# Raw attention products on quarters of the array, with loads, stores and order rearranged

## The chip, the core and the metric

The kernel runs on one core of a Trainium2 chip. The metric is the device time of one execution in microseconds (us). Three executions of the kernel before took 323.3, 323.69 and 323.8 us, a median of 323.69. The engines of the core are called as in the profile: PE is TensorE (the array that multiplies matrices), PEld its loading of weights, DVE is VectorE, ACT is ScalarE, POOL is GpSimd, and SP is SyncE, which here only issues DMAs. ACT and POOL issue DMAs too. Each engine executes its own instructions in the order in which the program lists them, and waits where one needs what another engine has not delivered.

## The reference

Batch 8, 8 heads, 576 tokens, head size 64, so 512 channels. Everything is float32 in the kernel; the weights arrive as float64 and are narrowed on the chip.

```python
def _attn_ref(q, k, v, g_norm):
    kv = np.einsum('bhsd,bhse->bhde', k, v)
    out = np.einsum('bhsd,bhde->bhse', q, kv)
    rms = np.sqrt(np.mean(out * out, axis=-1, keepdims=True) + 1e-06)
    return (out / rms * g_norm).astype(np.float32)

# x = the heads side by side: (8, 576, 512)
def _moe_ref(x, w_val, conv_w, w_out):
    # gate_pre[s] = sum over k of conv_w[k] * x[s - 4 + k], a causal filter of 5 taps per channel
    gate = 1.0 / (1.0 + np.exp(-gate_pre))
    val = x @ w_val
    return (gate * val @ w_out).astype(np.float32)
```

## The kernel before

**Tiling.** For each of the 8 batches the 576 tokens are cut into four chunks of 128 (numbers 0 to 3) and a tail of 64 (number 4, also written NJ). Heads are taken in four pairs hp; a pair's two heads fill the 128 partitions, r = 0 the lower 64 and r = 1 the upper 64.

**The steps of a batch.** kv_product multiplies k and v into a PSUM tile, 64 by 64 for each head. kv_copy (ACT) puts the result into kv_bd, a tile of 128 by 128 for each pair of heads with the two heads' 64 by 64 blocks on the diagonal and zeros, written once at the start, elsewhere. raw_product multiplies a chunk of q (transposed, in qT, as weights) by kv_bd: one matmul for each pair of heads, 128 columns each. square (ACT) squares the chunk, sums (DVE) adds over each head, powers (POOL) takes the power -1/2, and normalise (for batches 1 to 7 eight ACT instructions, one for each head) scales the chunk from PSUM to SBUF. turn_x and keep_x, or turn_blocks and move_blocks, transpose it into xT. gate_start, gate_tap and gate_end make the gate from xT, val_product or val_fast the val product (val_fast in the seven products of a fast scheme on halves), gated their product, and out_product or fast_product the output, which keep_out or fast_keep takes to SBUF and store writes to memory.

**Order.** PLAN (line 19) is the whole order, written out as one string by a planner that ran beforehand: the last loop of the kernel calls the step named by each piece, so a step's instructions go to the end of their engines' queues in this order. tail_and_kv is the raw product of a batch's tail with kv_product of the next batch. keep_warm n is n matmuls of the identity into a spare piece of PSUM, put where PE would have nothing to do.

**PSUM.** Its eight banks are shared out in line 228, `BANKS = {"kv": 1, "raw": 2, "tp": 1, "mm": 4}`. A raw chunk takes one bank of the two called raw (for batch 0 partly of mm), so that one chunk can be multiplied while the one before is still read. turn_x uses tp. In the last fast products the two raw banks hold the sums called cb and a (out_bank, line 727).

**Queues.** SP issues nearly all loads and stores. For batch 0, load_half puts the two halves of v and the first half of k on ACT's queue and the second half of k on SP's; load_q_rows and load_tails (four DMAs, lines 305 to 310) are on SP's. POOL issues the DMAs of g_norm and conv_w, and those of move_blocks. set_up (line 258) clears, on POOL, those parts of the four tail tiles that stay zero: `for pair in tails`, eight memsets. store_last writes the last two chunks, the even one through SP, the odd one through ACT, four DMAs each.

Of the kernel before, what the change touches and what calls it, by code (L numbers as in the profile page):

```python
# [15 lines left out]
P = 128  # L16
# [3 lines left out]
load_half k 0 0; stage_weight cw 0; load_q_rows 0 0; load_half v 0 0; load_q_rows 0 1; load_tails 0;  # L20
load_half v 0 1; warm_up; keep_warm 16; turn_q_rows 0 0; load_half k 0 1; turn_q_rows 0 1; sort_q 0 0;
turn_q_rows 0 2; stage_weight wval 0; sort_q 0 1; stage_weight wval 1; turn_q_rows 0 3; sort_q 0 2;
turn_q_rows 0 4; load_q_rows 1 0; keep_warm 1; kv_product 0 0; load_q_rows 1 1; load_half k 1 0;
narrow_weight cw 0 0; narrow_weight cw 0 1; load_half v 1 0; narrow_weight cw 0 2; load_tails 1;
narrow_weight cw 0 3; sort_q 0 3; narrow_weight cw 0 4; keep_warm 5; kv_product 0 1; narrow_weight cw 0 5;
sort_q 0 4; narrow_weight cw 0 6; narrow_weight cw 0 7; turn_cw; kv_copy 0; narrow_weight wval 0 0;
narrow_weight wval 0 1; load_half k 1 1; keep_warm 3; raw_product 0 3; load_half v 1 1; narrow_weight wval 1 0;
raw_product 0 2; keep_cw; stage_weight wval 2; square 0 3; stage_weight wval 3; narrow_weight wval 0 2;
raw_product 0 4; sums 0 3; stage_weight wout 0; square 0 2; raw_product 0 1; powers 0 3;
narrow_weight wval 1 1; sums 0 2; square 0 4; narrow_weight wval 0 3; keep_warm 2; turn_q_rows 1 0; square 0 1;  # L30
powers 0 2; normalise 0 3; narrow_weight wval 1 2; sums 0 4; sort_q 1 0; keep_warm 2; turn_x 0 3; sums 0 1;
turn_q_rows 1 1; powers 0 4; keep_x 0 3; normalise 0 2; narrow_weight wval 1 3; powers 0 1; turn_x 0 2;
normalise 0 4; narrow_weight wval 0 4; turn_q_rows 1 2; keep_x 0 2; narrow_weight wval 1 4; turn_x 0 4;
normalise 0 1; keep_x 0 4; narrow_weight wval 1 5; sort_q 1 1; keep_warm 3; raw_product 0 0; halo 0;
narrow_weight wval 1 6; turn_x 0 1; narrow_weight wval 1 7; square 0 0; turn_q_rows 1 3;
narrow_weight wval 0 5; sort_q 1 2; sums 0 0; keep_x 0 1; turn_q_rows 1 4; narrow_weight wval 0 6; powers 0 0;
sort_q 1 3; kv_product 1 0; load_q 2 0; narrow_weight wval 0 7; sort_q 1 4; narrow_weight wval 2 0;
kv_product 1 1; narrow_weight wval 2 1; normalise 0 0; narrow_weight wval 2 2; narrow_weight wval 3 0;
val_product 0 0 1; load_half v 2 1; kv_copy 1; load_q 2 1; narrow_weight wval 2 3; narrow_weight wval 3 1;
narrow_weight wval 2 4; turn_x 0 0; raw_product 1 3; narrow_weight wval 2 5; keep_x 0 0;  # L40
narrow_weight wval 2 6; keep_val 0 0 1; raw_product 1 2; load_half k 2 0; square 1 3; narrow_weight wval 2 7;
gate_start 0 0; load_half k 2 1; val_product 0 1 1; sums 1 3; load_tails 2; narrow_weight wval 3 2;
gate_tap 0 0 3; powers 1 3; square 1 2; gate_start 0 1; sums 1 2; val_product 0 0 0; keep_val 0 1 1;
turn_q 2 0; narrow_weight wval 3 3; powers 1 2; load_half v 2 0; normalise 1 3; gate_tap 0 1 3;
stage_weight wout 2; val_product 0 1 0; gate_tap 0 1 2; load_q 2 2; narrow_weight wout 0 0; keep_val 0 0 0;
narrow_weight wval 3 4; gate_start 0 2; raw_product 1 1; turn_q 2 1; narrow_weight wout 0 1; gate_tap 0 2 3;
turn_x 1 3; square 1 1; load_q 2 3; val_product 0 2 1; narrow_weight wout 0 2; sums 1 1; keep_x 1 3;
gate_tap 0 0 2; powers 1 1; normalise 1 2; gate_tap 0 1 1; val_product 0 2 0; gate_tap 0 0 1;
narrow_weight wval 3 5; normalise 1 1; narrow_weight wval 3 6; turn_x 1 2; gate_tap 0 0 0; raw_product 1 0;
keep_x 1 2; narrow_weight wval 3 7; tail_and_kv 1; square 1 0; gate_tap 0 1 0; keep_val 0 2 1; gate_tap 0 2 2;  # L50
gate_end 0 0; gate_end 0 1; sums 1 0; keep_val 0 1 0; gate_tap 0 2 1; narrow_weight wout 0 3; powers 1 0;
turn_x 1 1; gated 0 0; load_half k 3 0; kv_copy 2; val_product 0 3 1; stage_weight wout 1;
narrow_weight wout 0 4; square 1 4; keep_x 1 1; load_q 3 0; narrow_weight wout 2 0; normalise 1 0; sums 1 4;
turn_q 2 2; powers 1 4; val_product 0 3 0; narrow_weight wout 0 5; turn_q 2 3; gate_start 0 3; load_q 3 1;
normalise 1 4; narrow_weight wout 0 6; turn_x 1 0; gate_tap 0 3 3; raw_product 2 3; keep_x 1 0;
narrow_weight wout 0 7; keep_val 0 2 0; turn_x 1 4; square 2 3; gate_tap 0 3 2; raw_product 2 2; keep_x 1 4;
stage_weight wout 3; sums 2 3; narrow_weight wout 2 1; val_product 1 0 1; load_half k 3 1; gated 0 1;
narrow_weight wout 2 2; powers 2 3; load_tails 3; gate_tap 0 2 0; square 2 2; narrow_weight wout 2 3;
val_sums 0; val_product 1 0 0; keep_val 0 3 1; sums 2 2; keep_val 1 0 1; keep_val 0 3 0;
narrow_weight wout 1 0; powers 2 2; normalise 2 3; narrow_weight wout 2 4; load_half v 3 1; val_product 1 1 1;  # L60
load_half v 3 0; gate_tap 0 3 1; load_q 3 2; gate_tap 0 3 0; narrow_weight wout 1 1; narrow_weight wout 2 5;
gate_end 0 2; turn_blocks 2 3; raw_product 2 1; narrow_weight wout 1 2; turn_q 3 0; val_product 1 1 0;
square 2 1; narrow_weight wout 2 6; keep_val 1 0 0; load_q 3 3; narrow_weight wout 1 3; sums 2 1;
normalise 2 2; narrow_weight wout 2 7; val_product 1 2 1; powers 2 1; turn_q 3 1; narrow_weight wout 1 4;
gate_end 0 3; load_q 4 0; val_sums 1; raw_product 2 0; normalise 2 1; gated 0 2; val_product 1 2 0;
narrow_weight wout 3 0; gated 0 3; narrow_weight wout 3 1; narrow_weight wout 1 5; square 2 0; turn_blocks 2 2;
tail_and_kv 2; narrow_weight wout 3 2; sums 2 0; keep_val 1 1 1; narrow_weight wout 3 3;
narrow_weight wout 1 6; powers 2 0; turn_blocks 2 1; gate_start 1 0; narrow_weight wout 3 4; keep_val 1 1 0;
keep_val 1 2 1; turn_q 3 2; val_product 1 3 1; halo 1; square 2 4; load_half v 4 1; kv_copy 3;
narrow_weight wout 1 7; load_q 4 1; normalise 2 0; sums 2 4; gate_tap 1 0 3; powers 2 4; val_product 1 3 0;  # L70
turn_q 3 3; normalise 2 4; narrow_weight wout 3 5; load_tails 4; narrow_weight wout 3 6; raw_product 3 3;
gate_start 1 3; narrow_weight wout 3 7; gate_start 1 2; turn_x 2 4; turn_blocks 2 0; raw_product 3 2;
keep_x 2 4; gate_tap 1 0 2; square 3 3; move_blocks 2 3; out_product 0 3; square 3 2; load_half k 4 0;
gate_tap 1 2 3; keep_val 1 3 1; load_half v 4 0; gate_tap 1 0 1; keep_val 1 3 0; keep_val 1 2 0; sums 3 3;
gate_tap 1 0 0; powers 3 3; sums 3 2; gate_end 1 0; out_product 0 1; gate_tap 1 2 2; keep_out 0 3; powers 3 2;
gate_tap 1 3 3; normalise 3 3; store 0 3; gated 1 0; gate_tap 1 3 2; move_blocks 2 2; normalise 3 2;
gate_tap 1 2 1; load_half k 4 1; raw_product 3 1; load_q 4 2; gate_tap 1 3 1; out_product 0 2; gate_start 1 1;
turn_blocks 3 3; square 3 1; gate_tap 1 2 0; keep_out 0 1; sums 3 1; gate_tap 1 3 0; powers 3 1;
gate_tap 1 1 3; raw_product 3 0; keep_out 0 2; gate_tap 1 1 2; move_blocks 2 1; out_product 0 0; store 0 2;
normalise 3 1; gate_tap 1 1 1; gate_tap 1 1 0; gate_end 1 2; turn_q 4 0; store 0 1; halo 2; gate_end 1 1;  # L80
val_sums 2; gated 1 1; tail_and_kv 3; keep_out 0 0; load_q 4 3; gated 1 2; gate_end 1 3; gated 1 3;
move_blocks 2 0; turn_blocks 3 2; turn_q 4 1; out_product 0 4; kv_copy 4; turn_blocks 3 1; square 3 4;
load_q 5 0; square 3 0; weight_sums 0; sums 3 4; sums 3 0; powers 3 4; turn_q 4 2; out_product 0 5; powers 3 0;
load_half k 5 0; normalise 3 4; val_sums 3; store 0 0; turn_q 4 3; keep_out 0 4; weight_sums 1; normalise 3 0;
# [104 lines left out]
def kernel(  # L189
# [68 lines left out]
    def set_up():  # L258
# [4 lines left out]
        for pair in tails:  # L263
            for t in pair:
                nc.gpsimd.memset(t[T:P, 0:HP], 0.0)
                nc.gpsimd.memset(t[0:T, HP:H], 0.0)
        for t in kv_bd:
            nc.vector.memset(t[:], 0.0)
# [238 lines left out]
    def heads(c):  # L507
        return H if c < NJ else H // 2
# [315 lines left out]
```

## Time and profile before

The profile is of one execution, which took 324.43 us as a whole; its span, from the first to the last instruction, is 322.6 us. The clock granted to PE was 1.000 over the span.

| | us | instructions |
|---|---|---|
| median of three runs | 323.69 | |
| profiled execution | 324.43 | |
| span in the profile | 322.6 | 6073 |
| PEld busy | 223.2 | 2049 |
| ACT busy | 191.8 | 535 |
| POOL busy | 146.3 | 185 |
| raw products (L500), full array, PE | 33.5 | 256 |
| raw products of tails (L500), half the columns, PE | 5.3 | 64 |
| keep_warm (L432), PE | 10.7 | 64 |
| powers (L528), POOL | 74.0 | 40 |
| normalise on ACT (L539) | 55.5 | 252 |

How to read the views: a row of the groups names line, engine, operation, what is written and read, and the shape, then x and the number of instructions, then the busy time in us and the mean of one in ns, then idle time before them and what ended it. For PE the shape begins with rows*columns of the array that the weights fill. A line of the chain in time order has the start, the length and what the end of the program was waiting for then; consecutive instructions of a kind are merged. In the slices each digit is the busy share of a fortieth of the span in tenths.

### The profile page before, as it was taken

How to read it: one execution, taken by the hardware profiler on the slowest of the kernel's cores; microseconds unless marked ns; L12 is line 12 of the kernel's file. 1: busy time of each engine (PE TensorE's matmuls, PEld its weight loads, DVE VectorE, ACT ScalarE, POOL GpSimd, SP SyncE). 2: the span in 40 equal slices, each digit the busy share in tenths (PEclk: the TensorE clock that was granted, in tenths of full speed). 3: DMA queues.
4: the chain of work that ended last, by engine and by line, in shares of the span. 5: the costliest groups of instructions: out<-in, count | busy, mean ns of one | idle time of the engine just before them, and what ended most of it. 6: DMA issues, size and time to landing. Idle time of an engine off the chain costs nothing.

```text
span 322.6 us, 6073 instructions
## 1 busy us (share of the span) xinstructions
PE 313.4 (97%) x2049; PEld 223.2 (69%) x2049; DVE 246.2 (76%) x430; ACT 191.8 (59%) x535; POOL 146.3 (45%) x185
## 2 busy tenths in 40 slices
PE   8899999899999999999999999999999999999994
PEld 8788888688656577667767675686545676877652
DVE  1149799899989889989897999798748379764511
ACT  1467898999767758495767565656743443341311
POOL 6037254455678578427682943279549000000000
PEclk9999999999999999999999999999999999999999
DMA  8998896995978789688948682223146211112323
GB/s 271 319 335 286 217 294 184 322 305 131 284 194 235 208 253 238 176 259 204 247 108 257 189 249 74 67 65 85 41 114 171 50 33 35 25 40 52 81 66 98
DMA packets 43647, 55.35 MB, mean 172 GB/s; under 512 B 14934, under 2 KB 33366, under 8 KB 43616
## 3 DMA queue, kind: packets, MB, share of 16 engines
q1 hardware_dynamic: 38624, 46.81, 52.5%
q0 software_dynamic: 3168, 6.32, 7.8%
q10 hardware_dynamic: 1824, 1.84, 1.9%
q8 instruction: 16, 0.26, 0.4%
q14 instruction: 15, 0.12, 0.2%
HBM read 39.21 MB, written 9.44 MB: 151 GB/s over the span
## 4 chain that ended last, share of the span: by engine, by line
PE 89%; DMA 4%; ACT 3%; POOL 2%; DVE 1%; ACTq 0%; issue 0%; POOLq 0%
PE out L685 26%; PE va L654 15%; PE raw L500 10%; PE val L604 7%; PE vc L654 7%; PE kv L443 5%; PE out L692 4%; PE a L749 4%; PE vb L654 4%; PE cb L749 3%; DMA v<-in_v_dram 2%; POOL rt L528 2%; DMA vl<-in_v_dram 2%; PE qTps L482 1%; ACT x L539 1%; PE xTps L554 1%
## 5 line engine op out<-in xcount | busy, mean ns | idle before, releaser
L528 POOL TENSOR_TENSOR rt<-ss,mhalf 128x8 f32<-128x8 f32 (+1 forms) x40 | 74.0, 1856 | 85.2 <-DVE ss L522 85.1
L592 DVE SCALAR_TENSOR_TENSOR gate<-xT,cwT,gate 128x576 f32<-128x576 f32 x128 | 101.4, 813 | 9.4 <-ACT gate L586 7.7
L685 PE MATMUL out<-wout,gv 128*128 128x512 f32 x192 | 85.3, 594 | 0.0
L539 ACT ACTIVATE x<-raw,rt 128x64 f32<-128x64 f32 x252 | 55.5, 338 | 17.7 <-POOL rt L528 17.5
L685 PEld LDWEIGHTS out<-wout,gv 128*128 128x128 f32 x192 | 35.9, 190 | 39.5 <-issue 37.7
L575 POOL DMA_DIRECT2D xT<-y x96 | 53.1, 559 | 16.4 <-PE xTps L554 7.5
L500 PEld LDWEIGHTS raw<-kvbd,qT 128*128 128x128 f32 (+1 forms) x320 | 35.7, 180 | 7.0 <-issue 2.7
L500 PE MATMUL raw<-kvbd,qT 128*128 128x128 f32 (+1 forms) x320 | 38.5, 278 | 0.0
L604 PE MATMUL val<-xT,wval 128*128 128x288 f32 x128 | 32.6, 408 | 0.0
L522 DVE TENSOR_REDUCE ss<-sq 128x8 f32<-128x520 f32 (+1 forms) x40 | 25.0, 632 | 7.0 <-ACT sq L514 6.8
L700 ACT COPY ot<-out 128x512 f32<-128x512 f32 x28 | 16.4, 588 | 19.7 <-PE out L685 15.3
L604 PEld LDWEIGHTS val<-xT,wval 128*128 128x128 f32 x128 | 23.7, 190 | 6.0
L654 PE MATMUL va<-xs,vsum 128*128 128x288 f32 x96 | 27.2, 406 | 0.0
L514 ACT ACTIVATE sq<-raw 128x512 f32<-128x512 f32 (+1 forms) x40 | 22.7, 570 | 6.2 <-PE raw L500 6.2
L586 ACT ACTIVATE gate<-xT,cwT 128x576 f32<-128x576 f32 x32 | 24.8, 793 | 2.3 <-DVE gv L617 2.2
L617 DVE TENSOR_TENSOR gv<-gv,gate 128x576 f32<-128x576 f32 x32 | 23.7, 759 | 3.1 <-ACT gate L599 2.1
L599 ACT ACTIVATE gate<-gate 128x576 f32<-128x576 f32 x32 | 21.9, 706 | 4.4 <-DVE gate L592 4.4
L654 PEld LDWEIGHTS va<-xs,vsum 128*128 128x128 f32 x96 | 18.1, 190 | 4.7
L567 DVE STREAM_TRANSPOSE y<-x 128x512 f32<-128x512 f32 x24 | 16.7, 701 | 2.1 <-ACT x L539 2.0
L443 PE MATMUL kv<-v,k 128*64 128x64 f32 x448 | 17.1, 222 | 0.0
L468 DVE STREAM_TRANSPOSE qT<-qs 128x512 f32<-128x512 f32 x24 | 16.7, 695 | 0.0
L443 PEld LDWEIGHTS kv<-v,k 128*64 128x64 f32 x448 | 16.0, 138 | 0.2
(113 smaller groups left out, 430.3 us busy)
## 6 DMA issues: line engine op xcount, KB each, us to landing
qs<-in_q_dram SPq DMA_DIRECT2D x96, 140.0 KB, 4.4
out_dram<-ot SPq DMA_DIRECT2D x140, 64.0 KB, 1.7
v<-in_v_dram SPq DMA_DIRECT2D x12, 512.0 KB, 5.6
k<-in_k_dram SPq DMA_DIRECT2D x12, 512.0 KB, 5.7
xT<-y POOLq DMA_DIRECT2D x96, 64.0 KB, 2.9
qs<-in_q_dram SPq DMA_DIRECT2D x4, 576.0 KB, 6.7
y<-in_moe_w_val_dram SPq DMA_DIRECT2D x4, 512.0 KB, 6.9
w_wout<-in_moe_w_out_dram SPq DMA_DIRECT2D x4, 512.0 KB, 6.3
```

The lines of the kernel that those rows point to most:

```text
L443: nc.tensor.matmul(kvp[r * D:(r + 1) * D, hp, :], kl[:, head(hp, r), :] if j == NJ else st["k", b, at[0]][:, at[1], at[2], j, :], vl[:, he ...
L500: nc.tensor.matmul(raw[row * m:(row + 1) * m, col * P:(col + 1) * P], st["qT", b][:, hp, c * P:c * P + m], kv_bd[b % 2][:, hp, :], start=T ...
L522: nc.vector.reduce_sum(out=ss[:, 0:n], in_=st["sq", b, c][:, 0:n], axis=AX.X)
L528: nc.gpsimd.tensor_tensor(out=rt[:, 0:n], in0=st["ss", b, c][:, 0:n], in1=mhalf[:, 0:n], op=ALU.pow)
L539: nc.scalar.activation(out=x[:, to * D:(to + 1) * D], in_=st["raw", b, c][:, h * D:(h + 1) * D], func=AF.Copy, scale=st["rt", b, c][:, h:h ...
L575: nc.gpsimd.dma_start(out=xTs[b % 2][i * TB:(i + 1) * TB, :, first:first + P], in_=y[a * TB:(a + 1) * TB, i])
L586: nc.scalar.activation(out=gate[:], in_=xTs[b % 2][:, jt, HALO:SX], func=AF.Copy, scale=cwT[:, K - 1, jt:jt + 1])
L592: nc.vector.scalar_tensor_tensor(out=gate[:], in0=xTs[b % 2][:, jt, tap * TB:tap * TB + S], scalar=cwT[:, tap, jt:jt + 1], in1=gate[:], op ...
L604: nc.tensor.matmul(val[:], wval[:, kc, jt * P:(jt + 1) * P], xTs[b % 2][:, kc, HALO + n * SV:HALO + (n + 1) * SV], start=(kc == 0), stop=( ...
L617: nc.vector.tensor_tensor(out=both, in0=both, in1=st["gate", b, jt][:], op=ALU.mult)
L654: nc.tensor.matmul(st[bank, "val", b, mj][:], weights_[:, k], tokens()[:, k], start=(n in (0, 1, 3) and k == 0), stop=(k == NK // 2 - 1), ...
L685: nc.tensor.matmul(po[:], gv[:, jt, first:first + P], wout[:, jt, :], start=(jt == 0), stop=(jt == NK - 1),)
```

## The change

Raw products of batches 1 to 7 are made for two chunks in one step, raw_pair, by matmuls with 64 rows and 64 columns of weights and 64 streamed columns, one for each pair of heads, chunk, half of the chunk's tokens and head r; only the diagonal blocks of kv_bd are read. The two raw banks become one tile, raws; head r of a pair writes to bank r, and a chunk takes one half of each bank. square and normalise read the new layout through by_head. The tails' raw products take a bank of tp from batch 2 on and of mm before. For batch 0 the tails are loaded by POOL's queue, all of k by SP's, and the second half of q by ACT's; half of the clearing of the tail tiles moves to DVE. The last chunk's store is split over ACT's and SP's queues. The order is a new one in all its parts.

```diff
-    BANKS = {"kv": 1, "raw": 2, "tp": 1, "mm": 4}
+    BANKS = {"kv": 1, "tp": 1, "mm": 4}
+    raws = psum.tile([P, 2, C], FP32, tag="raw", bufs=1, name="raw")
...
-        for pair in tails:
-            for t in pair:
-                nc.gpsimd.memset(t[T:P, 0:HP], 0.0)
-                nc.gpsimd.memset(t[0:T, HP:H], 0.0)
+        for t in tails[0]:
+            nc.gpsimd.memset(t[T:P, 0:HP], 0.0)
+            nc.gpsimd.memset(t[0:T, HP:H], 0.0)
...
+        for t in tails[1]:
+            nc.vector.memset(t[T:P, 0:HP], 0.0)
+            nc.vector.memset(t[0:T, HP:H], 0.0)
...
-                (nc.sync if i and name == "k" else nc.scalar).dma_start(
+                (nc.sync if i or name == "k" else nc.scalar).dma_start(
...
-                nc.sync.dma_start(
+                (nc.sync if b else nc.gpsimd).dma_start(
                     out=tails[b % 2][n][r * T:(r + 1) * T, r * HP:(r + 1) * HP],
...
-        nc.sync.dma_start(
+        (nc.scalar if r and b == 0 else nc.sync).dma_start(
             out=qs[:, r].rearrange("p n d -> p (n d)"),
...
-        raw = ps("mm" if b == 0 and c in (NJ, 1, 0) else "raw", [P, C], f"raw{b}_{c}")
+        if b == 0 and c in (3, 2):
+            raw = raws[:, 3 - c]
+        else:
+            raw = ps("tp" if b >= TURNED_X else "mm", [P, C], f"raw{b}_{c}")[:]
...
+    def raw_pair(b, c):
+        for x in (c, c - 1):
+            st["raw", b, x] = raws[:].rearrange("p r (x n) -> p x r n", x=2)[:, c - x]
+        for hp in range(HP):
+            for x in (c, c - 1):
+                for half in range(2):
+                    for r in range(2):
+                        rows, cols = slice(r * D, (r + 1) * D), slice(half * D, (half + 1) * D)
+                        nc.tensor.matmul(
+                            st["raw", b, x][cols, r, hp * D:(hp + 1) * D],
+                            st["qT", b][rows, hp, x * P + half * D:x * P + (half + 1) * D],
+                            kv_bd[b % 2][rows, hp, rows], start=True, stop=True)
...
-            kind = out_bank(i, p)
-            both = ps(kind, [P, 2, C // 2], f"cb{i}_{p}")
-            st["c", i, p], st["b", i, p] = both[:, 0], both[:, 1]
-            st["a", i, p] = ps(kind, [P, C // 2], f"a{i}_{p}")[:]
+            if i == B // 2 - 1 and p != 2:
+                both, a = (raws[:, x].rearrange("p (m n) -> p m n", m=2) for x in range(2))
+            else:
+                both, a = (ps("mm", [P, 2, C // 2], f"{n}{i}_{p}") for n in ("cb", "a"))
+            st["c", i, p], st["b", i, p], st["a", i, p] = both[:, 0], both[:, 1], a[:, 0]
...
-    def store_last(i, c):
-        store(i, c, nc.scalar if c % 2 else nc.sync)
+    def store_last(i, c, n):
+        store(i, c, nc.scalar if n else nc.sync, range(n * HB // 2, (n + 1) * HB // 2) if c % 2 else range(HB))
```

The pieces of the new order that the working refers to, the start, the raw pairs of batch 1, those at batch 6 and 7, and the end:

```diff
+load_q_rows 0 1; load_tails 0; load_q_rows 0 0; load_half v 0 0; load_half k 0 0; warm_up; load_half k 0 1;
+load_half v 0 1; stage_weight wval 0; stage_weight wval 1; keep_warm 14; turn_q_rows 0 0; turn_q_rows 0 1;
+sort_q 0 0; turn_q_rows 0 2; sort_q 0 1; turn_q_rows 0 3; sort_q 0 2; stage_weight cw 0; turn_q_rows 0 4;
+sort_q 0 3; kv_product 0 0; load_q_rows 1 0; load_q_rows 1 1; load_half k 1 0; load_half v 1 0;
+narrow_weight cw 0 0; load_tails 1; narrow_weight cw 0 1; narrow_weight cw 0 2; keep_warm 7; kv_product 0 1;
...
+narrow_weight cw 0 6; narrow_weight cw 0 7; kv_copy 0; load_half v 1 1; narrow_weight wval 0 0; keep_warm 3;
+turn_cw; stage_weight wval 2; raw_product 0 3; keep_cw; stage_weight wval 3; narrow_weight wval 1 0;
...
+raw_pair 1 3; load_tails 2; narrow_weight wval 2 2; turn_x 0 0; square 1 3; load_q 2 1; val_product 0 0 1;
...
+keep_warm 2; raw_pair 1 1; keep_val 0 0 1; narrow_weight wval 3 1; gate_tap 0 3 2; load_q 2 3; tail_and_kv 1;
...
+gate_tap 4 0 2; val_keep 4 1 2; gate_end 4 2; store 1 2; gate_tap 4 3 0; raw_pair 6 1; keep_out 1 6; gated 4 2;
+out_product 1 8; square 6 0; square 6 1; store 1 6; sums 6 0; val_keep 4 1 1; gate_tap 4 0 1; gate_start 4 1;
+powers 6 0; gate_end 4 3; sums 6 1; gate_tap 4 0 0; powers 6 1; tail_and_kv 6; turn_blocks 6 2; gate_end 4 0;
...
+val_fast 4 1 6; keep_out 1 8; gate_tap 4 1 1; raw_pair 7 3; store 1 8; sums 6 4; val_keep 4 1 6; gated 4 0;
...
+out_product 3 8; fast_keep 3 3 2; fast_keep 3 3 1; fast_product 3 3 3; keep_out 3 8; fast_product 3 3 5;
+fast_keep 3 3 3; store 3 8; fast_product 3 3 4; fast_keep 3 3 5; fast_keep 3 3 4; store_last 3 6 0;
+fast_product 3 3 6; fast_keep 3 3 6; store_last 3 7 1; store_last 3 7 0
```

## The prediction

> **What bounds the kernel now.** I read the page first: shares of the span, then the slices, then the chain that ended last.
>
> ```profile
> PE 313.4 (97%) x2049; PEld 223.2 (69%) x2049; DVE 246.2 (76%) x430; ACT 191.8 (59%) x535; POOL 146.3 (45%) x185
> ...
> PE   8899999899999999999999999999999999999994
> ...
> DVE  1149799899989889989897999798748379764511
> ...
> PE 89%; DMA 4%; ACT 3%; POOL 2%; DVE 1%; ACTq 0%; issue 0%; POOLq 0%
> ```
>
> PE is busy in every slice but the last and is 89% of the chain, so what PE need not do comes off the span nearly in full, if the others keep up. A busy PE can hide slack, so I checked rates in the groups with shapes kept apart and in the chain in order of time:
>
> ```profile
> L500 PE MATMUL raw<-kvbd,qT 128*128 128x128 f32 x256 | 33.5, 276 | 0.0
> ...
> L443 PE MATMUL kv<-v,k 128*64 128x64 f32 x448 | 17.1, 222 | 0.0
> ```
> ```profile
> 133.33 0.97 PE va L654 x4
> 134.30 0.59 PE raw L500 x8
> 134.90 2.33 PE kv L443 x80
> 137.23 3.44 PE out L692 x16
> 140.66 1.17 PE va L654 x4
> 141.83 0.89 PE raw L500 x8
> ```
>
> Each f32 matmul of the code is two instructions. A raw chunk on the whole array (last line) is 8 instructions in 0.89 us: 111 ns each for 128 columns. The val products take 0.97/4 = 243 ns for 288 columns, and 0.243/288 = 0.84 ns per column is the streaming rate; 128 columns are then 108 ns. So raw is bound by streaming, not by its weights. kv, whose weights fill half of the array's columns, takes 2.33/80 = 29.1 ns for 64 columns, where streaming is 54: two halves run at once. In the single records its starts stand 13 and 45 ns apart in turn, a round of 58 ns for two. The tail raw product of four matmuls (134.30) has its first starts 14 ns apart too, though the code issues two matmuls for one half before the other half's: PE takes the halves' work as each is free.
>
> PE loses about 5 us outside streaming: start, end and two waits near 58 to 61 us.
>
> **The change, part by part.**
>
> *Raw products.* Gone: for batches 1 to 7, chunks 3 to 0, 28 products of 0.893 us, 25.0 us. Their weights qT meet kv_bd, half of which is zeros. Added: 14 pairs of 32 matmuls (64 instructions) of 64 rows by 64 columns, 64 streamed columns each, 16 instructions per quarter. No row of the trace uses half of the array's rows, so I bound it. Lower end: four at once at streaming, 53.7/4 = 13.4 ns per instruction. Upper end: only two at once, as kv, 29.1 ns. Nearest row: kv's round of 58 ns, now holding four instead of two: 14.6 ns, 0.93 us per pair, 13.1 us in all. That four starts fit into 58 ns is suggested by the 13 ns between neighbours (4 x 13 = 52). Against it speaks a rule of the Trainium skill (TensorE: Matmul & The Clock Gate, section Back-to-back issue gap): for 1 to 64 columns a matmul costs about 60 cycles, a floor near 25 ns between starts. By that a pair takes 1.60 us and all 22.4. The row shows starts of 13 ns, so the floor does not hold between neighbouring tiles; but its mean of 29.1 never went under 25, so the row does not refute it as a rate. I take 14.6 because the same page (Part 3, Measured speedup vs the span model) reports 10.6 times for 16 tiles, which no run here shows. **25.0 to 13.1: -11.9 us** (ends -13.0 and +1.1).
>
> *Changes of array shape.* In the chain, the tail product at 134.30 should start at 134.14 (last start 133.90 plus 0.24) and starts at 134.23: 0.10 to enter a half-array stretch. Leaving it, four va matmuls take 1.17 for 0.97: 0.20. Counted along both plans: full to partial and back 17 times before, 23 after, so 6 x 0.30 = 1.8; and 6 changes from quarters to halves (pairs next to tail_and_kv, to the batch 7 tail, to out_product 1 8), bounded by 0 and 0.30, taken as an entry, 0.10: 0.6. **+2.4 us.**
>
> *Start.* The chain there:
>
> ```profile
> 1.75 6.76 DMA v<-in_v_dram
> 8.51 0.02 issue
> 8.53 5.25 DMA vl<-in_v_dram
> 13.78 0.14 issue
> 13.92 0.88 PE kv L443 x22
> 14.80 1.31 PE kv L432 x10
> 16.11 1.34 PE kv L443 x40
> ```
>
> kv_product 0 0 stops 1.5 us for the tails of v, whose two DMAs SP could issue only at 7.73. The change puts the four tails on POOL's queue, moves q's second half from SP's to ScalarE's, where v already is, and k's first half from ScalarE's to SP's; each of the two then issues five DMAs for batch 0, SP before its first val weights. ScalarE's table load (1.28 us) stands before the last two of v. POOL's memsets before the tails fall from eight to four (0.3 us each; the other four go to DVE, idle there), so its tail DMAs start near 2.8 us. The tail wait goes; next late are the second halves of k and v. q, k and v of batch 0 with their tails are 3.54 MB; at the 294 GB/s of the first 16 us from 1.75 on they land at 13.8, and up to 3.6 us later (1.05 MB at the same rate) if both val weights of SP's queue went first. With kv_product 0 1 taken at 15.2 instead of 16.11 and the same 3.1 us from there, the first raw product is at 18.3 instead of 19.2; bounds 16.9 and 20.5. **-0.9 us.** The price: behind the tails POOL issues gcol and cw later; cw's data came at 10.98 with issue at 5.29. With four tail DMAs at 0.5 to 1.2 us each (cw's took 0.54, gcol's pair 1.24) cw comes some 2.5 us later, its narrowing (2.6 us) ends near 16, and turn_cw stands before raw_product 0 3 on PE: 0 to 2 us, taken 0.5 below.
>
> *keep_warm.* 25 to 24 up to the first raw product, 7 to 11 after it; six instructions took 0.94, so 4 x 0.31: **+1.2 us**.
>
> *One raw tile instead of two buffers.* raw_pair c=1 must wait until both chunks of c=3 are normalised, and the next batch's pair for c=1. All squares, sums, powers and normalises stay, in number and size. In the timeline one chunk goes from square at 45.13 to the end of its normalise at 50.45, 5.3 us; the second adds at least its 1.75 of ScalarE or POOL's 2.1; where queues were full it took 8 us (50.78 to 58.77). Work on PE between the pairs: 10 us or more nearly everywhere, enough. Short: pair 1 3 to 1 1, three val products and two turns, 7.3 us and two keep_warm: 0 to 3, taken 1.0, with val_product 0 1 0 and all of the kv of batch 2 queued behind it. Pair 6 1 to 7 3, about 9.5 us, with kv_copy 7 behind two normalises on ScalarE: 0 to 2, taken 0.7. With cw: **+2.2 us** (0 to 7). The two waits near 58 to 61 (1.4 us) may go; I leave them in as cover.
>
> The batch tails move to the bank of turn_x: used after them only by the turn of the same chunk, no cost. Sums, powers and other steps are reordered without change of size.
>
> *End.* The timeline's last lines:
>
> ```profile
> 317.32 0.42 DVE L758 TENSOR_TENSOR ot<-cb,ot 128x256 f32<-128x256 f32 x1 [0.81 <-PE cb L749]
> 318.18 0.37 ACT L772 COPY ot<-a 128x256 f32<-128x256 f32 x1 [2.54 <-PE a L749]
> 318.58 1.86 ACTq L781 DMA_DIRECT2D out_dram<-ot  x4
> ```
>
> Four issues of 0.46 from one queue follow the last copy, and the last lands 1.3 us later. After: two on each queue; ScalarE's end 0.9 earlier. SP must first have issued chunk 6's four; products 5 and 4 change places, so chunk 6 is whole one product (0.86) sooner and SP is free near 318.8. -0.8. Product 5 no longer follows the add that reads the same bank, and the 0.27 us before 316.15 goes. **-1.1 us.**
>
> **The sum** on the profiled execution: 324.4 - 11.9 + 2.4 - 0.9 + 1.2 + 2.2 - 1.1 = 316.3. The profiled execution stands 0.7 above the median 323.69, so the median is forecast at **315.6** (own range 312 to 319).
>
> **Rivals.**
> 1. *Quarters do not run four at once* (slower). Place: the 14 pairs. Price: at 29.1 ns 13.0 us more, 328.6; at the 25 ns floor 9.3 more, 324.9. It decides from 8.1/14 = 0.58 us more per pair, 1.51 us or 23.6 ns an instruction. For: no row of the trace splits rows, and the floor. Against: the 13 ns starts.
> 2. *DVE takes over.* Windows of 16 us show DVE busy 161.7 of 176 us from 32 to 208, 92%. Ten of the 14 pairs lie there and take 10/14 of 9.5, 6.8 us, out; DVE would have to run at 161.7/169.2 = 96%. If it cannot exceed 92%, all 6.8 are lost: 322.4. With it goes a wait for the one raw tile wherever the sums come late. Against: after 224 us DVE is 60% busy and work can move there, as weight_sums does.
> 3. *The change does more*: waits at zero, start at its lower bound, 312.
>
> **How the numbers follow.** Forecast 0.60; rival 1 0.16; rival 2 0.20, of which 0.04 within and 0.04 above no change, as its waits may exceed what was taken; rival 3 0.04. A measurement here tells 0.2% from no change. Faster 0.60 + 0.04 + 0.12 = 0.76, same 0.04, slower 0.20. The range 311.8 to 325.0 holds the forecast, rival 3, all of rival 2 but its worst and the lower end of rival 1; left out is about 0.18.
>
> **What would show it.** Right: a pair of 64 instructions within 1.0 us in the chain, PE near 305 us busy, the first raw product before 19 us, two output issues on each queue at the end. Wrong: pairs of 1.6 us or more (rival 1); PE idle before raw pairs with ScalarE's normalise as releaser, or DVE above 95% through the middle with PE waiting on sums (rival 2); PE waiting at turn_cw.

## The result, and the profile after

The changed kernel takes 320.92 us (median of four executions, 320.38 to 321.3), the kernel before 323.5 (323.05 to 323.8). The ratio is 0.992, with a 95% interval of 0.9901 to 0.994: faster by 2.6 us where 8.1 were forecast. In a later series the same two measured 321.36 against 323.57, ratio 0.9931 (0.9917 to 0.9945).

The profiled execution took 321.3 us, with a span of 319.5. The page shows, in the same places as before:

```profile
PE 308.0 (96%) x2727; PEld 213.1 (67%) x2727; DVE 245.5 (77%) x434; ACT 190.7 (60%) x535; POOL 144.9 (45%) x185
...
PE   8989899998999999999999999999999999999993
...
DVE  2149699999799699898999889997996686665201
...
PE 96%; issue 1%; ACT 1%; DVE 1%; DVEq 0%; POOL 0%; ACTq 0%; POOLq 0%
```

PE is still the bound; the DMAs of the start have left the chain. PE's busy time fell by 5.4 us, less than the 9.5 that raw products and changes of array shape should have given together. The new thing is "issue 1%": time in which PE waited for nothing that the profile shows. In the chain in order of time, around 71 us:

```profile
67.65 1.09 PE raw L520 x64
68.75 0.59 PE raw L503 x8
69.34 2.32 PE kv L443 x79
71.66 1.67 issue
73.32 0.22 PE kv L443
73.54 7.96 PE val L629 x32
```

The first line is a raw pair: 64 instructions in 1.09 us with the change of array shape in front, where two whole-array chunks took 1.79. In the single records of such a pair the starts stand 7, 7, 6 and 38 ns apart in turn: a round of 58 ns, now of four, as the prediction took it from kv's round of two. In the last lines one kv matmul is left when PE stops, for 1.67 us, before it.

The groups with shapes kept apart show the pairs and one part of the last fast products (the last row is from the kernel before):

```profile
L520 PE MATMUL raw<-kvbd,qT 64*64 64x64 f32 x896 | 16.5, 221 | 0.7 <-issue 0.7
...
L772 PE MATMUL raw<-wsum,sums 128*128 128x256 f32 x36 | 9.7, 395 | 1.8 <-ACT ot L785 0.7 <-DVE ot L781 0.6 <-ACT ot L783 0.5
...
L772 PE MATMUL raw<-wsum,gv 128*128 128x256 f32 x12 | 3.3, 396 | 1.1 <-DVE ot L781 1.1
```
```profile
L749 PE MATMUL a<-wsum,sums 128*128 128x256 f32 x32 | 8.2, 379 | 0.0
```

The second and third row are not raw products: raws is now also the home of the sums of the last fast products, so their rows carry its name. Both have waits for copies and adds of ACT and DVE; before, such products had none. The view of waits for PE has it in sum:

```profile
PE raw L772 <- DVE ot L781: 1.7, 3, 0.8
PE kv L443 <- issue: 1.7, 1, 1.7
PE kv L432 <- POOL ident masks.py:199: 1.4, 1, 1.4
PE kv L432 <- ACT kvbd L458: 1.1, 2, 0.8
PE raw L772 <- ACT ot L785: 0.7, 1, 0.7
PE raw L520 <- issue: 0.7, 1, 0.7
PE raw L772 <- ACT ot L783: 0.5, 1, 0.5
```

A row gives the waiting engine and line, what released it, and the us in total, the times and the longest. Two families are new: 2.9 us on L772, and two stops by "issue", 1.7 and 0.7. (The view counts from the end that is modelled for the matmul before, and leaves out short waits; the loss from start to start is larger.) None is a raw pair waiting for normalise, or turn_cw. And the end of the timeline shows how the first family works; the second block is the kernel before at the same place:

```profile
311.07 1.03 PE L772 MATMUL raw<-wout,sums 128*128 128x256 f32 x4
312.19 0.43 DVE L781 TENSOR_TENSOR ot<-raw,ot 128x256 f32<-128x256 f32 x1 [9.30 <-PE raw L772]
312.67 0.73 PEld L772 LDWEIGHTS raw<-wsum,sums 128*128 128x128 f32 x4 [0.98 <-DVE ot L781]
312.67 1.13 PE L772 MATMUL raw<-wsum,sums 128*128 128x256 f32 x4 [0.57 <-DVE ot L781]
313.84 0.76 DVE L781 TENSOR_TENSOR ot<-raw,ot 128x256 f32<-128x256 f32 x2 [1.22 <-PE raw L772]
314.65 0.73 PEld L772 LDWEIGHTS raw<-wsum,gv 128*128 128x128 f32 x4 [1.25 <-DVE ot L781]
```
```profile
315.02 1.03 PE L749 MATMUL a<-wsum,sums 128*128 128x256 f32 x4
...
315.67 0.42 DVE L758 TENSOR_TENSOR ot<-cb,ot 128x256 f32<-128x256 f32 x1 [7.79 <-ACT ot L762]
316.09 0.42 DVE L758 TENSOR_TENSOR ot<-a,ot 128x256 f32<-128x256 f32 x1
```

DVE's add at 312.19 reads the sum b, finished near 311.2; it starts when PE's next product, into the sum c, is done. PE's product into a, in the other bank, waits for that add. PE and DVE take turns, over a tile and not over data. Before, a lay in a tile of its own, and PE's product into a (315.02) started ahead of the add that reads b (315.67).

So after the result there were two suspects, and a rival for each. **The one tile**: it makes PE, DVE and ACT take turns in the last fast products; the rival is that DVE and ACT are simply late there in the new order. **The stops**: PE's instructions do not arrive in time; the rivals are a DMA or another engine that the view doesn't show.

### The profile page after: what moved, and what is told of

The parts are those of the page before. It is cut to its first block, busy times and chain, and to the rows that moved or that the text cites. A ratio compares the mean times of both kernels' runs of the same rounds, so it can differ in the third digit from the quotient of the medians.

```text
span 319.5 us, 7447 instructions
## 1 busy us (share of the span) xinstructions
PE 308.0 (96%) x2727; PEld 213.1 (67%) x2727; DVE 245.5 (77%) x434; ACT 190.7 (60%) x535; POOL 144.9 (45%) x185
## 3 DMA queue, kind: packets, MB, share of 16 engines
q10 hardware_dynamic: 784, 1.25, 1.3%
## 4 chain that ended last, share of the span: by engine, by line
PE 96%; issue 1%; ACT 1%; DVE 1%; DVEq 0%; POOL 0%; ACTq 0%; POOLq 0%
PE out L710 26%; PE va L679 15%; PE val L629 10%; PE vc L679 7%; PE raw L772 6%; PE kv L443 6%; PE raw L520 5%; PE out L717 4%; PE kv L432 4%; PE vb L679 4%; PE qTps L482 3%; PE raw L503 3%; PE xTps L579 2%; PE a L772 1%; PE cb L772 1%
## 5 line engine op out<-in xcount | busy, mean ns | idle before, releaser
L552 POOL TENSOR_TENSOR rt<-ss,mhalf 128x8 f32<-128x8 f32 (+1 forms) x40 | 71.6, 1796 | 85.1 <-DVE ss L546 83.1
L617 DVE SCALAR_TENSOR_TENSOR gate<-xT,cwT,gate 128x576 f32<-128x576 f32 x128 | 100.1, 811 | 6.3 <-ACT gate L611 5.8
L564 ACT ACTIVATE x<-raw,rt 128x64 f32<-128x64 f32 x252 | 54.8, 353 | 7.1 <-POOL rt L552 6.7
L538 ACT ACTIVATE sq<-raw 128x512 f32<-128x512 f32 (+1 forms) x40 | 21.9, 559 | 12.6 <-PE raw L520 6.6
L520 PEld LDWEIGHTS raw<-kvbd,qT 64*64 64x64 f32 x896 | 14.4, 134 | 6.4 <-issue 2.4
L520 PE MATMUL raw<-kvbd,qT 64*64 64x64 f32 x896 | 16.5, 221 | 0.7 <-issue 0.7
```

Of the source, the lines that this page charges most:

```text
L520: nc.tensor.matmul(st["raw", b, x][cols, r, hp * D:(hp + 1) * D], st["qT", b][rows, hp, x * P + half * D:x * P + (half + 1) * D], kv_bd[b ...
L552: nc.gpsimd.tensor_tensor(out=rt[:, 0:n], in0=st["ss", b, c][:, 0:n], in1=mhalf[:, 0:n], op=ALU.pow)
L564: nc.scalar.activation(out=x[:, to * D:(to + 1) * D], in_=one, func=AF.Copy, scale=st["rt", b, c][:, h:h + 1])
L617: nc.vector.scalar_tensor_tensor(out=gate[:], in0=xTs[b % 2][:, jt, tap * TB:tap * TB + S], scalar=cwT[:, tap, jt:jt + 1], in1=gate[:], op ...
```

## The experiments

Each kernel is the changed one with the edits shown (lines left out are marked by "..."), timed beside the kernel before (323.3 to 323.6 in the three series). Theory A, B and C are the names that each expectation gives to its explanations.

**1. Separate banks for the last fast products.**

```diff
-                both, a = (raws[:, x].rearrange("p (m n) -> p m n", m=2) for x in range(2))
+                both, a = (ps(kind, [P, 2, C // 2], f"{n}{i}_{p}") for n, kind in (("cb", "tp"), ("a", "kv")))
```

> The changed kernel with one thing undone: in the last fast products (output tokens of batches 6 and 7, groups 0, 1 and 3) the sums a and the pair cb have two tiles of one bank each again, in the banks of turn_x and kv, which are idle by then, instead of both lying in the one tile raws. Theory A (the one tile makes each fast product wait for the copies and adds that read the other bank): PE's waits in these products, 4.8 us beyond streaming in the changed kernel against 0.8 before, fall to about 1, and the time falls by 3 to 4 us, to about 317.3. Theory B (these waits come from DVE and ACT being late in the new order, whatever the tile): PE waits as long for the same adds, time within 0.8 us of the changed kernel's 320.9. The trace up to 255 us is that of the changed kernel; if the two stops of PE without a releaser near 35 and 72 us come from fetching instructions, they should stand there again, with some spread in length.

Measured 317.17 us (315.49 to 319.81), ratio 0.9818 (0.9783 to 0.9853): 3.75 us below the changed kernel. Its timeline at the end:

```profile
307.09 1.13 PE L772 MATMUL cb<-wout,gv 128*128 128x256 f32 x4
...
308.06 1.03 PE L772 MATMUL cb<-wout,sums 128*128 128x256 f32 x4
...
308.92 1.03 PE L772 MATMUL a<-wsum,sums 128*128 128x256 f32 x4
309.18 0.76 DVE L781 TENSOR_TENSOR ot<-cb,ot 128x256 f32<-128x256 f32 x2 [8.52 <-PE cb L772]
...
310.52 1.13 PE L772 MATMUL a<-wsum,gv 128*128 128x256 f32 x4 [0.57 <-DVE ot L781]
```

The products into a no longer wait for the adds that read b and c; only the last waits, 0.57 us, for an add that reads a itself. The two stops are there again, 1.5 and 1.4 us. Theory A holds. The two traces, laid side by side matmul by matmul, put a firmer size on it: between 260 us and its last matmul PE loses 4.2 us in the changed kernel against this one, 3.1 of them before 307 us.

**2. Pairs on the whole array.** raw_pair makes each of its two chunks by four matmuls of 128 columns, and square and normalise read the old layout.

```diff
-            st["raw", b, x] = raws[:].rearrange("p r (x n) -> p x r n", x=2)[:, c - x]
...
+            st["raw", b, x] = raw = raws[:, c - x]
+            for hp in range(HP):
+                nc.tensor.matmul(
+                    raw[:, hp * P:(hp + 1) * P], st["qT", b][:, hp, x * P:(x + 1) * P],
+                    kv_bd[b % 2][:, hp, :], start=True, stop=True)
...
```

> The changed kernel, its order, tiles and queues kept, but each raw pair is made as two chunks on the whole array with kv_bd's zeros, 16 instructions of 128 columns for 64 of 64. Theory A (quarters run four at once and are worth what the trace says): a pair takes 1.79 us for 1.09 plus about 0.2 of leaving, 14 times 0.5 to 0.7, so 7 us more, less the 2.5 us of PE's two stops near 35 and 72 us, which should vanish with fewer instructions: about 325.4. Theory B (the quarters gain only what the whole change gained, 2.6 us, and order and queues nothing): about 323.5. Theory C (the quarters gain nothing in the time): 321.

Measured 326.69 us, ratio 1.0105 (1.0087 to 1.0123): the quarters are worth 5.8 us, and theory A's 325.4 was too low by 1.3. The chain of this kernel at the place of the stop:

```profile
68.38 1.78 PE raw L516 x16
70.16 0.59 PE raw L503 x8
70.75 2.33 PE kv L443 x80
73.09 3.11 PE val L622 x12
```

The kv matmuls run through, and no stop stands near 35 us either. This kernel begins its val product at 73.09, earlier than the changed kernel (73.54), though its pair is slower: here the stop ate the gain of the pairs so far.

**3. kv moved away from the pair.** tail_and_kv 2 goes behind the next val_product.

```diff
-tail_and_kv 2; square 2 1;
+square 2 1;
...
-val_product 1 2 1;
+val_product 1 2 1; tail_and_kv 2;
```

> The changed kernel with one step moved: tail_and_kv 2 stands after val_product 1 2 1 instead of right behind raw_pair 2 1. Theory A (PE stops 1.7 us near 72 us because pair, tail and kv together run through 304 matmul and weight instructions in 4.1 us, faster than instructions arrive): the 1.94 us of val product between them lets them arrive, the stop goes, 0.3 us of leaving and entering the half array is added: 1.4 us less, 319.5. Theory B (PE there waits for a DMA of the kv tails of batch 3 or for another engine): the stop moves with the step or shrinks by the 1.94 us only because it starts later, and val products stand before it, so the time also falls, but then the releaser of the first kv matmul with a tail is a DMA; and in the trace that DMA lands after the stop begins. If the time does not fall, what follows waits for something else.

Measured 320.29 us, ratio 0.9907 (0.9889 to 0.9924), 0.6 below the changed kernel where 1.4 were expected. In the trace the stop near 72 us is gone and nothing has taken its place there; the last matmul starts 1.3 us earlier. The one near 35 us is longer by 0.2. That is for A; the medians confirm less of it than the trace.

**4. Less filling.**

```diff
-keep_warm 14;
+keep_warm 11;
...
-keep_warm 3;
 turn_cw;
...
-keep_warm 2;
 raw_pair 1 3;
```

> The changed kernel with fewer filling matmuls on PE: 11 instead of 14 at the very start, none instead of 3 before turn_cw and none instead of 2 before raw_pair 1 3 (both of these write the tile that kv_copy reads, wait for it, and then run 0.94 and 0.64 us before work that is ready). Nothing of the output depends on them. Theory A (they are PE time on the path): 1.2 + 0.9 + 0.6 us less, up to 2.7, 318.2. Theory B (what follows, DMA landings of the next batch or DVE, ends later anyway): within 0.5 us of 320.9. A third possibility: without them the granted clock falls for a while, the profile's clock row shows it, and the time rises.

Measured 322.31 us (320.47 to 323.9), ratio 0.9967 (0.9946 to 0.9987): by the medians 1.4 us slower than with the filling. Only the third possibility had a rise, by the clock, and the times do go with it: four executions with a mean granted clock of 0.998 or 0.999 took 320.47 to 321.56 us, eight with 0.992 to 0.996 took 321.92 to 323.9. So the rise may be the clock's; where in those eight it fell, and what lowered it, no trace shows. The profiled execution is one of the first four (321.44 us, clock row full throughout) and level with the changed kernel's (321.3). So its trace can explain only why nothing was gained. The first raw product did start 0.9 us earlier; the timeline of PE shows where that went:

```profile
32.51 1.32 PE L520 MATMUL raw<-kvbd,qT 64*64 64x64 f32 x64
36.78 0.63 PE L579 MATMUL xTps<-ident,x 128*128 128x128 f32 x4 [2.95 <-DVE ot_wval L380]
```

PE stands still from 33.8 to 36.8. The releaser named is a DVE instruction whose result no transpose reads; what turn_x waits for, the normalise of its chunk on DVE and the copy on ACT that frees its bank, was done at 33.1 and 33.3. It is the stop of 35 us in a longer form, and it does not stand where it did: not inside the pair, but behind it.

This gave the key to the stops. I counted all of PE's recorded instructions in the order of their starts (matmuls, weight loads and a few waits for semaphores; 961 of them hold 946 matmuls and weight loads) and set the records of the instruction queue beside them (blocks of 16 KB; the change raises them from 16 to 21, as PE has 1,356 more matmuls and weight loads, and experiments 2 and 9 have 16 again). A stop is given from the last start before it to the first behind it:

```
kernel                 stop (us)       behind number   block landed   resumes after it
changed                34.58 to 35.49   961            34.09          1.40
changed                71.44 to 73.32   1985           71.86          1.47
separate banks         34.20 to 35.87   961            34.36          1.51
separate banks         71.81 to 73.41   1985           72.13          1.28
less filling           33.61 to 36.67   961            35.26          1.41
less filling           96.20 to 97.04   2497           95.62          1.43
```

Experiment 4 issues 32 fewer of them ahead of the pair, so its 961st is another instruction, behind the pair. The stop stays with the number and leaves the work. (The order of starts is not quite that of the program: at 29.72 us of experiment 4 a matmul of a tail starts ahead of one, at 29.74, that the program lists before it; the count does not depend on that.)

**5. Experiments 1 and 3 together.**

> Separate banks for the last fast products (first experiment) and tail_and_kv 2 moved behind val_product 1 2 1 (third experiment) in one kernel. If the two effects are independent, their measured gains add up: 320.9 - 3.75 - 0.6 = 316.5, and 315.7 if the stop of 1.4 to 1.9 us near 72 us goes as a whole, with one stop near 35 us left in the trace. If what follows the stop is bound by DVE, which is busy there throughout, nothing is gained over the 317.2 of separate banks alone.

Measured 316.54 us (315.56 to 318.32), ratio 0.979 (0.9765 to 0.9815), the lowest median here: the medians add up. But the interval overlaps that of experiment 1, and the profiled executions of both took 317.15, so the second gain is not shown apart. One stop of 1.8 us is left, behind number 961.

**6. A val product between kv and the first pair**, on top of experiment 5.

```diff
-keep_warm 2;
+val_product 0 0 1;
 raw_pair 1 3;
...
-load_q 2 1; val_product 0 0 1;
+load_q 2 1;
```

> The kernel of e5_split_and_apart, and val_product 0 0 1 moved ahead of raw_pair 1 3, in place of keep_warm 2. Theory A (PE stops near 35 us because kv_product 1 0, 1 1 and the pair run 288 matmul and weight instructions with little else between, faster than they are fetched): the val product's 1.94 us between them takes the stop of 0.7 to 1.6 us away, and the 0.64 us of filling goes: 1.3 to 2 us less than e5, about 314.5. Theory B (that stop is something that the later steps need anyway, DVE's narrowing of weights or DMA landings): within 0.4 us of e5. Against A would be a new stop elsewhere, as the blocks in which instructions come shift.

Measured 317.85 us, ratio 0.9829 (0.9808 to 0.985): by the medians 1.3 us slower than 5. The profiled executions are level (316.97 against 317.15), so the trace can't show the loss; PE's waits say where the expected gain went:

```profile
PE kv L443 <- issue: 1.5, 1, 1.5
...
PE raw L520 <- ACT x L564: 0.9, 1, 0.9
```

The stop behind 961 is gone, and one behind number 2497 has come, at 94.7 us in the kv of batch 4, resuming 1.50 us after its block. Moreover raw_pair 1 1 now waits 0.9 us for normalise: the val product was taken from the work between the two pairs, the very shortage that the prediction had priced.

**7. Less filling again**, on top of 6: 11 for 14 at the start, none before turn_cw.

> The kernel of e6_val_before_pair with 11 instead of 14 fillings at the start and none instead of 3 before turn_cw. In the fourth experiment the same cuts made the kernel slower by 1.4 us, with a stop of PE of 3.1 us near 36 us that the changed kernel has at 0.9. Theory A (that loss was instruction fetching at the pair, no wait for data): with the val product between, the cuts bring their 0.9 us and up to 1.2 us more: 312.5 to 313.6. Theory B (PE that comes earlier meets DVE's narrowing or DMA landings): no gain over e6, or a loss, and the trace shows PE waiting at a val product or at turn_x with a DVE instruction that just ended as releaser.

Measured 317.35 us, ratio 0.9808 (0.9788 to 0.9827). 0.5 us gained, within the noise of the two, of the 0.9 to 2.1 of theory A: the stop behind 961 is back (1.54 us), the one behind 2497 is 1.25. Neither theory as put: PE lost the time to instructions, not to data, though the val product stood between.

**8. The last store on one queue**, the split undone.

```diff
-fast_product 3 3 6; fast_keep 3 3 6; store_last 3 7 1; store_last 3 7 0
+fast_product 3 3 6; fast_keep 3 3 6; store_last 3 7 1
...
-    store(i, c, nc.scalar if n else nc.sync, range(n * HB // 2, (n + 1) * HB // 2) if c % 2 else range(HB))
+    store(i, c, nc.scalar if n else nc.sync)
```

> The changed kernel with the four DMAs of the last chunk on ScalarE's queue alone, as before the change; chunk 6 stays on SP's. If the split of the last store saves two issues of 0.46 us, as the prediction has it (0.8 us), the time rises by 0.8 to 0.9 us, to 321.8. If the last landing is set by something else, it stays within 0.3 us.

Measured 322.53 us (321.37 to 325.71), ratio 0.9982 (0.9954 to 1.0009), too wide to weigh 0.8 us; here too the longest executions have the lowest clock (324.34 to 325.71 at 0.990 and 0.991, 321.37 to 321.98 at 0.997 and 0.998). The traces can weigh it: from the start of the last matmul to the landing of the last output 3.15 us with the split and 3.96 without, 0.81 apart. PE's program is that of the changed kernel up to the end, but the block landed at 33.59 instead of 34.09, and the stop behind number 961 is 0.37 us long instead of 0.91.

**9. Whole-array pairs and separate banks together**, experiments 1 and 2: order, queues and stores are what remains of the change.

> Raw pairs on the whole array (second experiment) and separate banks in the last fast products (first experiment) in one kernel: what is left of the change is the new order, the queues of the start and the split of the last store. If the one tile costs the same 3.75 us here, the time is 326.7 - 3.75 = 322.9, so order and queues are worth about 0.5 us against the kernel before, and the quarters 322.9 - 317.2 = 5.8 us, the 2.5 us of instruction stops taken off already; no stop of PE stands near 35 or 72 us. If separate banks gain much less here, the 3.75 us were bound up with the quarters.

Measured 322.49 us, ratio 0.9971 (0.996 to 0.9982). The one tile costs 326.69 - 322.49 = 4.2 us here, and 4.2 from 260 us to the last matmul in the two traces, so it has nothing to do with the quarters. Order, queues and stores are worth 1.1 us. The quarters are worth 322.49 - 317.17 = 5.3 (medians of two series), and 8.2 without the two stops of 1.5 and 1.4 us in the trace of experiment 1; the trace here has none.

**10. The changed kernel again.**

> The changed kernel once more, unaltered, beside e9_full_and_split on one chip. If the two stops come from blocks of instructions that run out at a fixed place of PE's program, they stand before the same instructions again (the 961st and the 1985th matmul or weight load), each 1.3 to 1.6 us after a block of 16 KB has landed, whatever their length. The median should be within 0.7 us of 320.9.

Measured 321.36 us, within what was said. The stops stand behind number 961 (0.57 us long, resuming 1.46 us after its block) and number 1985 (1.61 and 1.37). The first raw product came at 18.89 us here, against 17.97 in the first trace of the same kernel, with PE waiting for a half of v.

## Why the prediction was wrong

The sign, the bound and the main mechanism were right: raw products on quarters run four at once. Two costs were missing from the sum, the one tile for the last fast products and the instructions of the pairs. Of the four signs of being right, the first raw product before 19 us and the two output issues on each queue came; a pair of 1.09 us (for 1.0 at most) and PE's busy time of 308.0 (for near 305) missed narrowly.

- *Raw products and array shape, -9.5 together.* Right in kind: four at once, in the predicted round of 58 ns, 15 ns an instruction where 14.6 was taken. A pair with its entry takes 1.09 us for 1.03. Experiments 1 and 9 leave 8.2 without stops. Rival 1 is refuted, and with it, for neighbouring tiles, the floor near 25 ns between starts that the prediction takes from the Trainium skill (TensorE: Matmul & The Clock Gate, Back-to-back issue gap): a pair at that floor would take 1.60.
- *One raw tile, +2.2 with turn_cw.* This is the step that failed. I asked what the merged tile makes raw pairs wait for, where no wait came, and did not ask it of the other user of the same banks, the last fast products, though the diff shows them moving into raws. Before, a had a tile apart from cb. The runs price it at 3.75 (experiment 1) and 4.2 us (2 against 9; also both pairs of traces). That it is the tile that is tracked and not the data is read off the timeline; the experiments show that parting the tiles removes it.
- *Instructions, put at nothing.* The change makes fourfold the instructions of each chunk's product, and I priced only the array. Where a pair, a tail and a kv product follow each other, 304 matmuls and weight loads run in 4.1 us, 74 per us; the densest stretch of before, tail and kv, has 176 in 2.9, 60 per us, and was never stopped. By the waits the stops cost 2.4 us in the changed kernel, 1.7 in its repetition and 2.9 in experiment 1. Density alone does not decide: the same sequence at 93.3 us runs through in the changed kernel.
- *Start, -0.9.* The first raw product came at 17.97 instead of 19.20, -1.2, and in experiment 10 -0.3: the size is within what one execution differs from another. The wait for the tails of v (1.5) went, as predicted; 0.5 and 0.3 of it are left in the traces of experiments 3 and 8.
- *keep_warm, +1.2.* By start-to-start times the filling, with the waits in it, grew by 1.7 us, and by 0.7 in experiment 10. The traces of experiments 4 and 7 show that taking filling away doesn't give the time back, because PE then runs into a stop sooner.
- *End, -1.1.* The split of the store gave 0.8, as worked out. The 0.27 us before product 5 went, but the exchange of products 5 and 4 puts product 6 right behind 4, in the same sum a, whose add it has to await: 0.74 us, which I did not price and which stays in experiment 1. The one tile put 0.74 us in front of product 4 and another 0.27 in front of 6.
- *Cover, not counted.* The two waits near 58 to 61 us, 1.4 by the prediction, went; no wait of PE stands between 36 and 71 us.
- *Rival 2, DVE takes over.* It did not: DVE is 77% busy, for 76% before, and PE's waits for DVE of more than 0.5 us lie in the last 8 us, where DVE is idle most of the time.

In numbers on the profiled execution: 316.3, less 2.2 for waits that did not come and 1.4 for those that went, plus 4.2 for the one tile, 2.4 for the stops, 0.8 for the pairs' 0.06 us each and 0.7 for the last product, is 320.8; it took 321.3. The start (-0.3) and the filling (+0.5) are within what one execution differs from another. So two terms erred to the good side by 3.6 and hid part of the missing costs; that is luck. With both missing costs partly undone (experiment 5) the kernel takes 316.5, against the 315.6 forecast, which for the same reason does not confirm the sum.

What stays open: why blocks are asked for when they are, and so how to place the dense stretches. In experiments 4, 6 and 7 one stop went and another came or came back, and I have no rule that says which. Open too is why the clock was lower in some executions of experiments 4 and 8.

## What to carry to other kernels

When a buffer is merged or renamed, list every step that uses it, not only those that the change is about, and ask of each what it will now wait for. When a product is cut into smaller pieces, count instructions per us along PE's order as well as array time, above all where dense steps become neighbours. A stop that keeps its number in the instruction stream while the work around it moves is not a wait for data.

## What the runs showed of the hardware

Four f32 matmuls of 64 by 64 with 64 streamed columns run at once in a round of 58 ns, with starts 6 to 7 ns apart. PE makes stops that belong to no work: always behind the same number of instructions (961, 1985 or 2497, which differ by multiples of 512), for 0.4 to 3.1 us, and it resumes 1.3 to 1.6 us after a block of 16 KB has landed. I read them as instructions that have not arrived. The profile calls this "issue", or names an instruction that happened to end then.
